# Float64 weights to float32 on VectorE and ScalarE, and exponentials with a per-partition bias, in an mLSTM cell with a GELU feed-forward block

## The chip, the cores and the metric

The kernel runs on one core of one Trainium2 chip. The metric is the device time of one execution in microseconds (us), the median of several runs. Five engines work side by side, each through its own list of instructions in order: TensorE (PE: matmuls, with weight loads in a row of their own, PEld), VectorE (DVE), ScalarE (ACT), GpSimd (POOL) and SyncE (SP). SP does no arithmetic here; it issues DMAs. They wait for one another by semaphores.

## The reference, cut to what matters

```python
# q, k, v, o_gate: (4, 8, 768, 40); i_gate, f_gate: (4, 8, 768); w_in (320, 2048), w_out (2048, 320) in float64
for t in range(S):
    m_new  = np.maximum(f[:, :, t] + m, i[:, :, t])
    f_stab = np.exp(f[:, :, t] + m - m_new)
    i_stab = np.exp(i[:, :, t] - m_new)
    m = m_new
    C = f_stab * C + i_stab * outer(v_t, k_t)          # 40 x 40 for each batch and head
    n = f_stab * n + i_stab * k_t
    y[:, :, t] = sigmoid(o_t) * (C @ q_t) / max(abs(n @ q_t), 1)
x = y as (4 * 768 tokens, 320)
out = gelu_exact(x @ w_in) @ w_out                     # float32
```

## The kernel before, in words

The 768 tokens of each of 4 batches are cut into 6 chunks of 128. A *token tile* is one chunk of one batch, 128 tokens on the partitions, 8 heads beside each other. With `M_t` the running maximum of the chunk and `a_s` the gate of token s less the sum of the forget gates, a token s weighs `exp(a_s - M_t)` for a token t at or after it.

The start (lines 126 to 182) computes `a` and `M` with one row a head, writes `M` to DRAM (`M_d`, line 164) and reads it back broadcast to all partitions, one token tile at a time (`load_M`, tile `Mb`, 512 KB, three buffers). Transposes on PE turn `a` into `aT`, tokens on the partitions.

Then come 6 chunks. Each has a *cell stage* (`cell_steps`) and a *feed-forward block*: the *up stage* (`up_steps`, line 358: 16 blocks `f` of 3 matmuls each, then GELU on ACT into `g`) and the *down part* (`down_steps`, line 371, 16 pieces of 4 matmuls). The function `weave` spreads the steps of one list between those of another: the down part of chunk c is woven into the cell stage of chunk c + 1. That is the order in which instructions stand on each engine; no engine changes its order at run time.

The cell stage has for each batch b: `turn` (k and q transposed on PE into `pt`, copied by ACT to `kT` and `qT`), `scores` (PE `ps`, then DVE multiplies `ps` by the weights `W`, line 289; PE `pf`, `pc`; the state), `values` (PE `ph`, DVE and POOL make `y`; then `load` fetches a later tile), `turn_y` (`y` transposed into `xT`, the input of the up stage). They run with a lag of one step from each to the next.

The weights `W` are made in two functions outside the steps. `distances` (line 246), ahead of the up stage, subtracts on DVE (line 251), masks on POOL (line 253) and loads the next `M`. `activations` (line 257), ahead of the cell stage, takes the exponentials of 4 token tiles (ACT, 128x1024 each, line 260) and the sigmoids of 4 output gates (line 263).

The feed-forward weights come in float64 and become float32 from their bits, in pieces (`convert`, line 212): 12 pieces of `w_in` of up to 128x512, woven into the first cell stage, and 16 of `w_out` of 128x320, woven into the first up stage. A piece takes one ACT instruction (line 222), three on POOL (lines 223 to 225) and five on DVE (lines 227 to 234). `fetch` brings the bits in, two buffers:

```python
nc.scalar.activation(out=s, in_=hf, func=AF.Abs)
nc.gpsimd.tensor_scalar(out=s, in0=s, scalar1=TINY, scalar2=None, op0=OP.is_ge)
nc.gpsimd.tensor_tensor(out=s, in0=s, in1=hf, op=OP.mult)
nc.gpsimd.tensor_scalar(out=s, in0=s, scalar1=-HUGE, scalar2=HUGE, op0=OP.max, op1=OP.min)
```

Of the kernel before, what the change touches and what calls it, by code (L numbers as in the profile page):

```python
# [36 lines left out]
def kernel(  # L37
# [32 lines left out]
    WP = 512  # L70
# [6 lines left out]
    outp = ctx.enter_context(tc.tile_pool(name="outp", bufs=3))  # L77
# [115 lines left out]
    def weight_steps():  # L193
        """What brings w_in and w_out in, a piece of at most WP columns a step."""
# [17 lines left out]
        def convert(i):  # L212
# [33 lines left out]
    def distances(c):  # L246
        """M_t - a_s for the chunk's weights exp(a_s - M_t); beyond the diagonal, what gives 0."""
        for b in range(B):
            n = c * B + b
            W[n] = wts.tile([P, H, L], F32, name="W", tag="W")  # L250
            nc.vector.tensor_tensor(out=W[n], in0=Mb.pop(n), in1=per_head(aT, c, b).to_broadcast([P, H, L]),  # L251
                                    op=OP.subtract)
# [172 lines left out]
```

## Time and profile before

| what | value |
|---|---|
| time, median of 3 runs | 833.14 us (832.2 to 833.54) |
| span of the profiled execution | 830.5 us, from its first instruction to its last |
| what lies around the span | 2.6 us, the median less the span |
| PE busy | 674.7 us, 81% of the span |
| DVE, ACT, POOL busy | 240.7, 170.4, 199.5 us |
| chain of work that ended last | PE 67%, POOL 13%, issue 11%, ACT 5% of the span |

The chain is followed back from the last instruction: at each step to what released it. Granted clock is what the throttle gave TensorE, as a share of 2.4 GHz; its other level is 1.2 GHz, 0.50. Idle time of an engine that is not the bottleneck costs nothing, so what counts is where PE stands still and what ends each of its waits.

### The profile page before, as it was taken

To read this page: it belongs to the slowest core of one execution; us is meant where nothing else is said; L and a number is where in the kernel's file an instruction comes from. 1 tells how busy PE (TensorE), PEld (TensorE's weight loads), DVE (VectorE), ACT (ScalarE), POOL (GpSimd) and SP (SyncE) were. 2 spreads that over 40 slices of the span, in tenths; PEclk is the share of its full clock that TensorE was granted. 3 is DMA by queue.
4 is the path that set the end of the run, shared out by engine and by line. 5 is a ranking of instruction groups with operands and counts; after the bars stand their busy time and mean duration, and the time that the engine had idled before them with its cause. 6 is when DMAs were issued, how large, how long until landed. Compare 5 with 4: busy or idle time off the path is not lost.

```text
span 830.5 us, 7094 instructions
## 1 busy us (share of the span) xinstructions
PE 674.7 (81%) x2714; PEld 394.8 (48%) x2714; DVE 240.7 (29%) x438; ACT 170.4 (21%) x288; POOL 199.5 (24%) x214
## 2 busy tenths in 40 slices
PE   2136424477579999799999799997999997999998
PEld 1125321122258733388533587333885335773365
DVE  4257554455534320034400144200344001330000
ACT  1411002111330022510223300225102234012200
POOL 2276654766612130011300021300113000000000
PEclk9975556788879999999999899998999998999999
DMA  9944371522204540024500035400221000000000
GB/s 141 248 80 95 66 120 29 148 64 63 63 9 66 79 110 0 0 41 66 133 23 1 6 64 82 109 0 1 41 40 41 1 0 9 9 17 0 0 9 24
DMA packets 132208, 43.47 MB, mean 52 GB/s; under 512 B 101104, under 2 KB 128752, under 8 KB 132176
## 3 DMA queue, kind: packets, MB, share of 16 engines
q1 hardware_dynamic: 132176, 43.04, 25.7%
q8 instruction: 21, 0.34, 0.2%
q14 instruction: 11, 0.09, 0.0%
HBM read 38.99 MB, written 4.03 MB: 52 GB/s over the span
## 4 chain that ended last, share of the span: by engine, by line
PE 67%; POOL 13%; issue 11%; ACT 5%; DVE 1%; DMA 1%; SPq 0%; POOLq 0%; ACTq 0%
PE pu L358 28%; PE po L371 25%; POOL sig L225 4%; PE ph L321 4%; POOL sig L223 4%; POOL sig L224 3%; PE ps L286 3%; PE pf L293 3%; ACT W L260 2%; PE pt L273 2%; PE pc L305 2%; POOL W L253 1%; ACT ob L263 1%; PE px L341 1%; ACT L263 1%
## 5 line engine op out<-in xcount | busy, mean ns | idle before, releaser
L358 PE MATMUL pu<-xT,w_in 128*128 128x512 f32 (+1 forms) x576 | 296.2, 646 | 36.4 <-ACT g L359 20.8
L371 PE MATMUL po<-w_out,g 128*128 128x320 f32 x768 | 228.5, 445 | 0.0
L358 PEld LDWEIGHTS pu<-xT,w_in 128*128 128x128 f32 (+1 forms) x576 | 96.6, 193 | 233.2 <-issue 189.8
L371 PEld LDWEIGHTS po<-w_out,g 128*128 128x128 f32 x768 | 143.6, 196 | 51.2 <-issue 5.0
L289 DVE TENSOR_TENSOR W<-ps,W 128x512 f32<-128x512 f32 x48 | 30.9, 685 | 293.5 <-PE ps L286 293.5
L359 ACT ACTIVATE g<-pu 128x512 f32<-128x512 f32 x96 | 57.1, 594 | 187.2 <-PE pu L358 187.2
L314 POOL TENSOR_TENSOR state<-state,dec 64x164 f32<-64x164 f32 x32 | 14.7, 461 | 241.5 <-PE pf L293 240.3
L273 PE MATMUL pt<-ident,kb 128*128 128x128 f32 x96 | 19.2, 335 | 60.5 <-ACT kT L276 60.5
L328 POOL TENSOR_TENSOR y<-hs,ob 128x320 f32<-128x320 f32 x24 | 19.3, 805 | 189.0 <-DVE hs L324 164.8
L321 PEld LDWEIGHTS ph<-vb,W 128*128 128x128 f32 x384 | 53.0, 215 | 4.0 <-PE px L341 0.8
L321 PE MATMUL ph<-vb,W 128*128 128x41 f32 x384 | 51.7, 300 | 0.4 <-PE px L341 0.4
L305 PE MATMUL pc<-vw,kb 128*128 128x82 f32 x160 | 24.9, 306 | 32.2 <-POOL vw L300 32.2
L253 POOL TENSOR_SCALAR_AFFINE_SELECT W<-W 128x1024 f32<-128x1024 f32 x24 | 37.2, 1571 | 56.9 <-DVE W L251 56.9
L273 PEld LDWEIGHTS pt<-ident,kb 128*128 128x128 f32 x96 | 14.1, 173 | 69.3 <-ACT kT L276 63.5
L223 POOL TENSOR_SCALAR sig<-sig 128x320 f32<-128x320 f32 (+2 forms) x28 | 34.8, 1243 | 47.0 <-ACT sig L222 47.0
L225 POOL TENSOR_SCALAR sig<-sig 128x320 f32<-128x320 f32 (+2 forms) x28 | 44.3, 1582 | 2.5
L251 DVE TENSOR_TENSOR W<-Mb,aT 128x1024 f32<-128x1024 f32 x24 | 33.3, 1425 | 26.0 <-DMA Mb<-M_d 26.0
L227 DVE TENSOR_SCALAR pow<-sig 128x320 uint32<-128x320 uint32 (+2 forms) x28 | 15.2, 543 | 86.3 <-POOL sig L225 86.2
L305 PEld LDWEIGHTS pc<-vw,kb 128*128 128x128 f32 x160 | 22.7, 219 | 33.3 <-POOL vw L300 33.3
L374 ACT COPY o_sb<-po 128x320 f32<-128x320 f32 x24 | 10.2, 425 | 132.3 <-PE po L371 132.3
L276 ACT COPY kT<-pt 128x512 f32<-128x512 f32 x24 | 13.9, 579 | 106.5 <-PE pt L273 106.5
L222 ACT ACTIVATE sig<-bits 128x320 f32<-128x320 f32 (+2 forms) x28 | 15.6, 563 | 97.4 <-DMA bits<-in_moe_w_out_dram 66.3
(71 smaller groups left out, 453.9 us busy)
## 6 DMA issues: line engine op xcount, KB each, us to landing
Mb<-M_d SPq DMA_DIRECT2D x24, 512.0 KB, 5.3
bits<-in_moe_w_out_dram SPq DMA_DIRECT2D x16, 320.0 KB, 2.9
bits<-in_moe_w_in_dram SPq DMA_DIRECT2D x8, 512.0 KB, 3.8
qb<-in_q_dram SPq DMA_DIRECT2D x24, 160.0 KB, 4.1
kb<-in_k_dram SPq DMA_DIRECT2D x24, 160.0 KB, 4.2
vb<-in_v_dram SPq DMA_DIRECT2D x24, 160.0 KB, 4.2
ob<-in_o_gate_dram SPq DMA_DIRECT2D x24, 160.0 KB, 3.8
out_dram<-o_sb SPq DMA_DIRECT2D x24, 160.0 KB, 1.9
```

Of the source, the lines that this page charges most:

```text
L223: nc.gpsimd.tensor_scalar(out=s, in0=s, scalar1=TINY, scalar2=None, op0=OP.is_ge)
L224: nc.gpsimd.tensor_tensor(out=s, in0=s, in1=hf, op=OP.mult)
L225: nc.gpsimd.tensor_scalar(out=s, in0=s, scalar1=-HUGE, scalar2=HUGE, op0=OP.max, op1=OP.min)
L251: nc.vector.tensor_tensor(out=W[n], in0=Mb.pop(n), in1=per_head(aT, c, b).to_broadcast([P, H, L]), op=OP.subtract)
L253: nc.gpsimd.affine_select(out=W[n], in_=W[n], compare_op=OP.is_ge, fill=1.0e4, base=0, pattern=[[0, H], [1, L]], channel_multiplier=-1)
L273: nc.tensor.transpose(pt[:, p, :], src[n % NLD][:, 2 * p:2 * p + 2, :].rearrange("p h d -> p (h d)"), ident)
L289: nc.vector.tensor_tensor(out=w, in0=ps[hip], in1=w, op=OP.mult)
L305: nc.tensor.matmul(pc[:, p, :], kb[n % NLD][:, m, :].rearrange("p h d -> p (h d)"), vw[:, m, :].rearrange("p h d -> p (h d)"), start=True, ...
L321: nc.tensor.matmul(ph[:, h, :], Pm[b][:, h, :], vb[n % NLD][:, h, :], start=True, stop=True)
L358: nc.tensor.matmul(pu, w_in[0:w, cc, m], xT[0:w, cc, :], start=(cc == 0), stop=(cc == 2))
L359: nc.scalar.activation(out=g[:, f, :], in_=pu, func=AF.Gelu)
L371: nc.tensor.matmul(po, g[:, f, b * L:(b + 1) * L], w_out[:, f, :], start=(f == 0), stop=(f == NF - 1))
```

## The change

The conversion of a piece leaves POOL. The sign, the exponent and the significand are now taken from the bits by DVE (lines 224, 229, 231, 232, 234 of the changed kernel), and the exponent is shifted and clamped by two Relu instructions on ACT whose bias is a column of constants (lines 226 and 227). A piece of `w_in` is up to 1024 columns wide, so there are 6 of them; those of `w_out` stay 128x320. The first chunk of `M` is written as soon as it is there, by a DMA that ACT issues, and ACT also issues the first three `load_M`. `distances` and `activations` are gone: `weights_of` masks `Mb` in place on POOL and takes the exponential of each head (128x128) with `aT` as the bias of its partition, and its step, as that of the sigmoids, stands behind the first `turn` of the cell stage. In the first chunk each sigmoid stands in `values`. The loads of `q`, `k`, `v` and `o_gate` of the first tiles are spread between the weights' fetches, and `o_sb` has 2 buffers in place of 3.

```diff
-    WP = 512
+    WP = 1024
-    for n in range(B):
-        load(n)
+    nc.vector.memset(e_hi, 1151.0 * I23)
+    nc.vector.memset(e_lo, 255.0 * I23)
...
+        if c == 0:
+            nc.scalar.dma_start(out=M_d[:, 0:L], in_=M[:, 0])
+            for n in range(NM):
+                load_M(n, nc.scalar)
-    nc.sync.dma_start(out=M_d, in_=M.rearrange("p c l -> p (c l)"))
-    for n in range(NM):
-        load_M(n)
+    nc.scalar.dma_start(out=M_d[:, L:S], in_=M[:, 1:NCH].rearrange("p c l -> p (c l)"))
...
-            nc.scalar.activation(out=s, in_=hf, func=AF.Abs)
-            nc.gpsimd.tensor_scalar(out=s, in0=s, scalar1=TINY, scalar2=None, op0=OP.is_ge)
-            nc.gpsimd.tensor_tensor(out=s, in0=s, in1=hf, op=OP.mult)
-            nc.gpsimd.tensor_scalar(out=s, in0=s, scalar1=-HUGE, scalar2=HUGE, op0=OP.max, op1=OP.min)
-            nc.vector.tensor_scalar(out=pu, in0=su, scalar1=3, scalar2=0x3F800000,
-                                    op0=OP.logical_shift_left, op1=OP.bitwise_and)
-            nc.vector.scalar_tensor_tensor(out=pu, in0=su, scalar=0xC0000000, in1=pu,
-                                           op0=OP.bitwise_and, op1=OP.bitwise_or)
-            nc.vector.tensor_scalar(out=su, in0=su, scalar1=0xFFFFF, scalar2=0x100000,
+            nc.vector.tensor_scalar(out=pu, in0=hi, scalar1=20, scalar2=0x7FF,
+                                    op0=OP.logical_shift_right, op1=OP.bitwise_and)
+            nc.scalar.activation(out=p, in_=pu, func=AF.Relu, scale=-I23, bias=e_hi[0:w])
+            nc.scalar.activation(out=pu, in_=p, func=AF.Relu, scale=-1.0, bias=e_lo[0:w])
+            nc.vector.tensor_scalar(out=su, in0=hi, scalar1=0xFFFFF, scalar2=0x100000,
                                     op0=OP.bitwise_and, op1=OP.bitwise_or)
             nc.vector.scalar_tensor_tensor(out=s, in0=lo, scalar=2.0 ** -32, in1=su, op0=OP.mult, op1=OP.add)
+            nc.vector.scalar_tensor_tensor(out=pu, in0=hi, scalar=0x80000000, in1=pu,
+                                           op0=OP.bitwise_and, op1=OP.bitwise_or)
             nc.vector.scalar_tensor_tensor(out=dst, in0=s, scalar=2.0 ** -20, in1=p, op0=OP.mult, op1=OP.mult)
             fetch(i + 2)
+            if i < n_in and i % 2 == 0:
+                load(3 + i // 2)
...
+    def weights_of(n):
+        c, b = divmod(n, B)
+        W[n] = wts.tile([P, H, L], F32, name="W", tag="W")
+        M_n = Mb.pop(n)
+        nc.gpsimd.affine_select(out=M_n, in_=M_n, compare_op=OP.is_ge, fill=1.0e30, base=0,
+                                pattern=[[0, H], [1, L]], channel_multiplier=-1)
+        for h in range(H):
+            nc.scalar.activation(out=W[n][:, h, :], in_=M_n[:, h, :], func=AF.Exp, scale=-1.0,
+                                 bias=aT[:, c, b * H + h:b * H + h + 1])
+        load_M(n + NM)
...
+            if t == 0:
+                steps.append(lambda: [weights_of(c * B + b) for b in range(B)])
+                if c > 0:
+                    steps.append(lambda: [output_gate(c * B + b) for b in range(B)])
```

How the order on the engines moves, at three places. First ACT at the start of the program. Before:

```order
L172 ACT_TABLE_LOAD
L172 ACTIVATE ew<-ew 32x640
L173 ACTIVATE gg<-gg 32x640
L260 ACTIVATE W<-W 128x1024 x4
L263 ACT_TABLE_LOAD
```

and in the changed kernel (`pow` is the exponent's buffer in `convert`):

```order
L164 DMA M_d<-M 32x128
L122 DMA Mb<-M_d 128x8x128 x3
L170 DMA M_d<-M 32x640
L175 ACT_TABLE_LOAD
L175 ACTIVATE ew<-ew 32x640
L176 ACTIVATE gg<-gg 32x640
L277 COPY kT<-pt 128x512
L277 COPY qT<-pt 128x512
L259 ACTIVATE W<-Mb,aT 128x128 x32
```

The DMAs of `M` and the first copies of `kT` and `qT` now stand ahead of the exponentials; the sigmoids (with their table load) have gone to a later place.

Second, ACT where an up stage (16 GELUs) ends and a later cell stage begins. Before:

```order
L359 ACTIVATE g<-pu 128x512 x16
L260 ACT_TABLE_LOAD
L260 ACTIVATE W<-W 128x1024 x4
L263 ACT_TABLE_LOAD
L263 ACTIVATE ob_122<-ob_122 128x320
```

and in the changed kernel:

```order
L369 ACTIVATE g<-pu 128x512 x16
L277 COPY kT<-pt 128x512
L277 COPY qT<-pt 128x512
L259 ACT_TABLE_LOAD
L259 ACTIVATE W<-Mb,aT 128x128 x32
L264 ACT_TABLE_LOAD
```

The copies of batch 0 come first, and 32 small exponentials stand where 4 large ones did; the copies of batch 1 still stand behind all of them and the sigmoids.

Third, PE at the start of the second cell stage (`kb`, `qb`: the loaded k and q of one token tile). Before:

```order
L273 MATMUL pt<-ident,kb_112 128x128 x4
L273 MATMUL pt<-ident,qb_106 128x128 x4
L371 MATMUL po<-w_out,g 128x320 x4
L273 MATMUL pt<-ident,kb_113 128x128 x4
L273 MATMUL pt<-ident,qb_107 128x128 x4
L371 MATMUL po<-w_out,g 128x320 x4
L286 MATMUL ps<-qT,kT 128x128 x8
```

and in the changed kernel:

```order
L274 MATMUL pt<-ident,kb_114 128x128 x4
L274 MATMUL pt<-ident,qb_108 128x128 x4
L381 MATMUL po<-w_out,g 128x320 x8
L274 MATMUL pt<-ident,kb_115 128x128 x4
L274 MATMUL pt<-ident,qb_109 128x128 x4
L381 MATMUL po<-w_out,g 128x320 x4
L289 MATMUL ps<-qT,kT 128x128 x8
L296 MATMUL pf<-state_100,qT 128x82 x4
L308 MATMUL pc<-vw,kb_114 128x82 x4
L381 MATMUL po<-w_out,g 128x320 x4
L274 MATMUL pt<-ident,kb_110 128x128 x4
```

Two groups of the down part, not one, now stand between the first two `turn`s, since the two new steps draw one each. The `pt` buffers are two, so each `turn` waits until ACT has copied the one before it out.

## Rows read from the trace of the kernel before

**Rows 1.** Busy time by stage: stretch, length, PE, PEld, DVE, ACT, POOL, clock, DMA, GB/s.

```profile
39.80:136.10 96.30, 35.95 (x189) 32.13 (x188) 56.31 (x95) 10.28 (x19) 58.90 (x41) 0.57 0.47 83
136.10:215.90 79.80, 58.94 (x96) 18.48 (x96) 39.64 (x70) 16.35 (x32) 52.93 (x47) 0.81 0.29 84
215.90:291.60 75.70, 61.58 (x366) 48.48 (x366) 32.13 (x66) 16.05 (x28) 19.60 (x26) 0.91 0.30 51
291.60:338.80 47.20, 47.20 (x97) 15.30 (x95) 3.85 (x3) 10.66 (x17) 6.41 (x5) 1.00 0.18 48
338.80:405.30 66.50, 60.46 (x366) 47.85 (x366) 21.54 (x46) 15.18 (x26) 9.46 (x16) 0.97 0.29 48
...
348.10:350.20 2.10, 2.08 (x9) 2.09 (x10) 0.00 (x0) 1.06 (x3) 0.00 (x0) 0.50 0.00 0
```

**Rows 2.** Groups by line and shape in the first cell stage, 39.8 to 136.1 us.

```profile
L225 POOL TENSOR_SCALAR sig<-sig 128x512 f32<-128x512 f32 x8 | 16.1, 2010 | 0.7
...
L231 DVE TENSOR_SCALAR sig<-sig 64x512 uint32<-64x512 uint32 x3 | 1.3, 419 | 0.1
```

**Rows 3.** Timeline in the first up stage: start, length, engine, line; one piece of `w_out`.

```profile
178.68 0.67 DVE L233 SCALAR_TENSOR_TENSOR sig<-bits,sig 128x320 f32<-128x320 uint32 x1
...
179.87 0.33 DVE L227 TENSOR_SCALAR pow<-sig 128x320 uint32<-128x320 uint32 x1
180.23 0.49 DVE L229 SCALAR_TENSOR_TENSOR pow<-sig,pow 128x320 uint32<-128x320 uint32 x1
...
182.41 0.48 ACT L222 ACTIVATE sig<-bits 128x320 f32<-128x320 f32 x1 [6.73 <-DMA bits<-in_moe_w_out_dram]
```

**Rows 4.** Timeline of the start: `M`, the gates on ACT, `pt`, and SP's DMAs.

```profile
5.67 0.47 DVE L160 TENSOR_TENSOR_SCAN M<-a,m 32x128 f32<-32x128 f32 x1
...
11.07 0.74 ACT L173 ACTIVATE gg<-gg 32x640 f32<-32x640 f32 x1
...
14.63 1.06 PE L273 MATMUL pt<-ident,qb 128*128 128x128 f32 x4
...
17.07 1.09 SPq L164 DMA_DIRECT2D M_d<-M  x1
20.66 11.18 SPq L123 DMA_DIRECT2D Mb<-M_d  x7
```

**Rows 5.** Timeline where the second up stage ends and a cell stage begins.

```profile
338.93 0.60 ACT L359 ACTIVATE g<-pu 128x512 f32<-128x512 f32 x1 [2.37 <-PE pu L358]
...
339.76 2.32 PE L371 MATMUL po<-w_out,g 128*128 128x320 f32 x8
340.84 3.89 ACT L260 ACTIVATE W<-W 128x1024 f32<-128x1024 f32 x4
...
346.05 1.55 ACT L263 ACTIVATE ob<-ob 128x320 f32<-128x320 f32 x4
347.50 0.56 ACT L276 COPY kT<-pt 128x512 f32<-128x512 f32 x1
...
348.12 1.11 PE L273 MATMUL pt<-ident,kb 128*128 128x128 f32 x4 [6.04 <-ACT kT L276]
```

**Rows 6.** Single lines and one tile over the whole span: lengths in ns; `Mb`'s landing in us.

```profile
L343 ACT COPY xT<-px x24: 258/258/260, 91.7 to 743.7; 64x128 f32<-64x128 f32 x24
...
L251 DVE TENSOR_TENSOR W<-Mb,aT x24: 1209/1220/2108, 24.6 to 639.1; 128x1024 f32<-128x1024 f32 x24
...
L253 POOL TENSOR_SCALAR_AFFINE_SELECT W<-W x24: 1086/1092/3150, 25.9 to 640.4; 128x1024 f32<-128x1024 f32 x24
...
DMA to landing us min/median/max: 3.7/5.3/8.0
```

**Rows 7.** Timeline of DVE in the first cell stage: what one batch takes beside the conversion.

```profile
80.98 1.28 DVE L289 TENSOR_TENSOR W<-ps,W 128x512 f32<-128x512 f32 x2
82.18 0.65 DVE L311 COPY state<-pc 64x164 f32<-64x164 f32 x2
...
89.12 0.50 DVE L326 COPY hs<-ph 128x328 f32<-128x328 f32 x1
...
91.28 0.42 DVE L342 COPY xT<-px 128x256 f32<-128x256 f32 x1
```

More of the change, by code (lines that the diff above doesn't have):

```diff
@@ L15 @@
 P = 128
-TINY = 3.4332275390625e-05
-HUGE = 122879.9921875
+I23 = 2.0 ** 23
 def weave(main, fill):
@@ L76 @@
     two = ctx.enter_context(tc.tile_pool(name="two", bufs=2))
-    outp = ctx.enter_context(tc.tile_pool(name="outp", bufs=3))
+    outp = ctx.enter_context(tc.tile_pool(name="outp", bufs=2))
     dram = ctx.enter_context(tc.tile_pool(name="dram", bufs=1, space=bass.MemoryType.DRAM))
@@ L90 @@
     ident = const.tile([P, P], F32, name="ident")
+    e_hi = const.tile([P, 1], F32, name="e_hi")
+    e_lo = const.tile([P, 1], F32, name="e_lo")
     last = const.tile([P, P], F32, name="last")
@@ L115, with load_M @@
     Mb, W = {}, {}
-    def load_M(n):
+    def load_M(n, eng=nc.sync):
         if n >= NCH * B:
@@ L122, in load_M @@
         Mb[n] = wts.tile([P, H, L], F32, name="Mb", tag="Mb", bufs=NM)
-        nc.sync.dma_start(out=Mb[n], in_=M_d[b * H:(b + 1) * H, c * L:(c + 1) * L]
-                          .unsqueeze(0).to_broadcast([P, H, L]))
+        eng.dma_start(out=Mb[n], in_=M_d[b * H:(b + 1) * H, c * L:(c + 1) * L]
+                      .unsqueeze(0).to_broadcast([P, H, L]))
     nc.sync.dma_start(out=f_sb.rearrange("p c l -> p (c l)"), in_=f_gate.rearrange("b h s -> (b h) s"))
     nc.sync.dma_start(out=i_sb.rearrange("p c l -> p (c l)"), in_=i_gate.rearrange("b h s -> (b h) s"))
-    for t in qb[0:B] + kb[0:B]:
+    load(0)
+    for t in kb[0:B] + qb[0:B]:
         nc.gpsimd.memset(t[:, :, D:DP], 0.0)
@@ L216, in convert @@
             lo, hi = x[:, :, 0], x[:, :, 1]
-            hf = hi.bitcast(F32)
-            s = raw.tile([P, WP], F32, name="sig", tag="sig")[0:w, 0:n]
+            s = raw.tile([P, WP], F32, name="sig", tag="sig", bufs=1)[0:w, 0:n]
             p = raw.tile([P, WP], F32, name="pow", tag="pow")[0:w, 0:n]
             su, pu = s.bitcast(U32), p.bitcast(U32)
-            nc.scalar.activation(out=s, in_=hf, func=AF.Abs)
-            nc.gpsimd.tensor_scalar(out=s, in0=s, scalar1=TINY, scalar2=None, op0=OP.is_ge)
-            nc.gpsimd.tensor_tensor(out=s, in0=s, in1=hf, op=OP.mult)
-            nc.gpsimd.tensor_scalar(out=s, in0=s, scalar1=-HUGE, scalar2=HUGE, op0=OP.max, op1=OP.min)
-            nc.vector.tensor_scalar(out=pu, in0=su, scalar1=3, scalar2=0x3F800000,
-                                    op0=OP.logical_shift_left, op1=OP.bitwise_and)
-            nc.vector.scalar_tensor_tensor(out=pu, in0=su, scalar=0xC0000000, in1=pu,
-                                           op0=OP.bitwise_and, op1=OP.bitwise_or)
-            nc.vector.tensor_scalar(out=su, in0=su, scalar1=0xFFFFF, scalar2=0x100000,
+            nc.vector.tensor_scalar(out=pu, in0=hi, scalar1=20, scalar2=0x7FF,
[3 more added lines that the diff above has]
+            nc.vector.tensor_scalar(out=su, in0=hi, scalar1=0xFFFFF, scalar2=0x100000,
                                     op0=OP.bitwise_and, op1=OP.bitwise_or)
             nc.vector.scalar_tensor_tensor(out=s, in0=lo, scalar=2.0 ** -32, in1=su, op0=OP.mult, op1=OP.add)
+            nc.vector.scalar_tensor_tensor(out=pu, in0=hi, scalar=0x80000000, in1=pu,
+                                           op0=OP.bitwise_and, op1=OP.bitwise_or)
             nc.vector.scalar_tensor_tensor(out=dst, in0=s, scalar=2.0 ** -20, in1=p, op0=OP.mult, op1=OP.mult)
             fetch(i + 2)
+            if i < n_in and i % 2 == 0:
+                load(3 + i // 2)
         fetch(0)
+        load(1)
         fetch(1)
+        load(2)
         steps = [lambda i=i: convert(i) for i in range(len(pieces))]
@@ L244, in per_head, with output_gate @@
         return t[:, c, b * H:(b + 1) * H].unsqueeze(2)
[L246 to L252, printed above, removed]
-            nc.gpsimd.affine_select(out=W[n], in_=W[n], compare_op=OP.is_ge, fill=1.0e4, base=0,
-                                    pattern=[[0, H], [1, L]], channel_multiplier=-1)
-            load_M(n + NM)
-    def activations(c):
-        for b in range(B):
-            n = c * B + b
-            nc.scalar.activation(out=W[n], in_=W[n], func=AF.Exp, scale=-1.0)
-        for b in range(B):
-            t = ob[(c * B + b) % NLD]
-            nc.scalar.activation(out=t, in_=t, func=AF.Sigmoid)
+    def weights_of(n):
[8 more added lines that the diff above has]
+        load_M(n + NM)
+    def output_gate(n):
+        nc.scalar.activation(out=ob[n % NLD], in_=ob[n % NLD], func=AF.Sigmoid)
     def cell_steps(c):
@@ L279, in scores @@
             n = c * B + b
+            if n not in W:
+                weights_of(n)
             Pm[b] = W.pop(n)
@@ L318, in values @@
             n = c * B + b
+            if c == 0:
+                output_gate(n)
             ph = ps_h.tile([P, H, D1], F32, name="ph", tag="h")
@@ L377, in down_steps @@
         return [lambda b=b, f=f: part(b, f, f + 4) for b in range(B) for f in range(0, NF, 4)]
-    distances(0)
     in_steps, out_steps = weight_steps()
-    for n in range(B, NLD):
-        load(n)
-    activations(0)
     weave(cell_steps(0), in_steps)
     for c in range(NCH):
-        if c + 1 < NCH:
-            distances(c + 1)
         g = gp.tile([P, NF, TG], F32, name="g", tag="g")
@@ L390 @@
         if c + 1 < NCH:
-            activations(c + 1)
             weave(cell_steps(c + 1), down_steps(c, g))
```

## The prediction

> **What bounds the kernel now.** I read the stages first [rows 1], since a share over the whole span hides where the time lies. An up stage in its steady form is PE and nothing else: 47.2 us, all busy, clock 1.00. The first up stage takes 79.8 us for the same work, and the first cell stage 96.3 us with PE busy for 36.0 at a mean clock of 0.57. In both POOL is the busiest of the others, 58.9 and 52.9 us. The groups say with what: one of POOL's three conversion instructions alone takes 2.01 us for 512 columns [rows 2]. In the chain of waits these stages go through POOL's conversion and the waits around it, one piece behind the other. Later cell stages (five; the first of them 75.7 us, the others some 66.5) have one hole each: PE waits 6.04 us for ACT's copy of `kT`, because exponentials and sigmoids stand ahead of it [rows 5], and then runs 2.1 us at clock 0.50, the 1.2 GHz level [rows 1]. So the change meets three places: the way to the first up matmul (136.15 us into the span), the first up stage, and the holes.
>
> **The way to the first up matmul.** The chain is now on ACT, then DVE.
> - The scan of the first chunk of `M` ends at 6.14 [rows 4]. Before, `M_d` was issued at 17.07 and the first `Mb` could follow at 20.66, 3.6 us later. From 6.2 that puts the first `Mb` at 9.8; three issues by ACT at up to 1.1 each and the second `M_d` keep ACT until about 12.5. A table load of 1.3 (the gap from the GELU's end to the first exponential [rows 5]) and `ew`, `gg` at 0.74 each give 15.3; before, `gg` ended at 11.81 and the second `pt` at 15.69, 3.9 later, so 19.2 now, and two copies of 0.56 end at 20.3. The first `Mb` lands 3.7 to 8.0 us after its issue [rows 6], POOL masks it in 1.09: 14.6 to 18.9, covered.
> - An exponential of 128 columns has no row. Bounds: a copy of 64x128 takes 0.258 alone [rows 6]; an eighth of the 1024-wide one is 0.12 and a 320-wide sigmoid, back to back, 0.39 [rows 5]. I take 0.26, the same width: 2.1 a token tile. The fourth tile needs a buffer of the three, so its `Mb` is issued when the first tile's exponentials end (22.4), lands a median 5.3 later, is masked by 28.8, and its exponentials end at 30.9; those of tiles 2 and 3 lie inside. Copies of the second batch 1.1, then the two Relus of piece 0, by the 1024-wide rate of 3.89/4 and some 0.1 for the hand-over 1.06 each: 34.1. DVE, which did its first steps meanwhile, goes on here.
> - From there DVE is in order and the bound. The last two instructions of piece 0 at 1.22 (a two-source operation 1024 wide [rows 6]): 2.4. Four batches at 1.85 for scores and state and 2.58 from `hs` to the end of `xT` [rows 7]: 17.7. Pieces 1 to 4: a bit operation with one source took 0.33 us for 320 and 0.42 for 512 columns [rows 2, 3], about 0.7 for 1024; then the Relus 2.2 with the hand-over, with two DVE instructions beside them; then 2.4: 5.5 each, 22.0. If reading every second word costs the one-source operation its rate, it takes 1.22 and a piece 6.2. I take 5.5 and keep 6.2 for the range. PE runs its `ps` and `pc` between these at half clock, and DVE waits for it at batch 1 and 2; 3 us. ACT's last `xT` 0.3. Sum: 34.1 + 2.4 + 17.7 + 22.0 + 3 + 0.3 = 79.5, some 56.5 us earlier.
>
> The Trainium skill, VectorE: DVE Perf Modes, What auto-detection actually checks, lets a single-source operation run two elements a cycle if source and destination are in SBUF, and names no stride; by it a piece is the 5.5. No row here has a strided one.
>
> **The first up stage.** PE needs 47.2. The clock is low before it; 2.1 us at half rate [rows 1] cost 1.1. A piece of `w_out` on DVE and ACT: 0.33 to 0.49 for the first instruction, two Relus of 0.48 to 0.55, two DVE instructions of 0.49 [rows 3] and five hand-overs of under 0.1: 2.6 to 2.9, and a buffer of bits comes back 3.06 us after it is freed (179.35 to 182.41 [rows 3]) for every two pieces. PE's block of three matmuls takes 47.2/16 = 2.95, so PE is the bound, by little; 1.5 us for friction. 49.8 against 79.8: 30.0 earlier. POOL's 52.9 us there fall away with no heir on the path.
>
> **The holes.** Count from the end of an up stage. ACT: the GELU ends at 0.7 [rows 5], copies of batch 0 1.1, table 1.3, four tiles of exponentials; the fourth `Mb` is again issued behind the first tile (at 5.2), lands at 10.5, is masked at 11.6, and its exponentials end at 13.7. Then 2.8 for the table and sigmoids (344.73 to 347.50 [rows 5]) and the copy: 17.1. PE meanwhile has two `turn`s of 0.94 (338.83 to 339.76 for the first), four groups of the down part at 2.2 [rows 5], `ps`, `pf`, `pc` 2.9: 13.6 before it needs that copy. So the wait is 3.5 in place of 6.04; part of it moves forward, to `pc`, as POOL's `vw` now stands behind the fourth mask. The slow clock behind it I leave as it is, 1.1. That is 2.5 for each of the four later cell stages, 10. The second cell stage is 75.7 long, 9.2 over the steady 66.5, for ACT was held by the last conversion; now the last two Relus hold it for 1.0. Gain 9.2 - 1.0 + 2.5 = 10.7.
>
> **Other edits.** SP's four `Mb` loads stand ahead of bits 2 and the fourth tile's loads, so these wait for ACT until 30.9; they are needed on DVE and PE from about 45 on. Two `o_sb` buffers suffice, as the four copies are a group of several us apart from the landing. DVE's `distances` lay beside an up stage bound by PE and cost nothing before.
>
> **Sum.** 56.5 + 30.0 + 10 + 10.7 = 107.2. The profiled span is 830.5, with 2.6 to the median: 833.1 - 107.2 = 725.9; I say 726.
>
> **The rivals.**
> - *Small exponentials are dear* (0.39 each, the sigmoid's price). Tiles take 3.1; in a hole ACT reaches the copy at about 19, PE waits 5.4 and the gain there is 0.6 at most: 9.5 less over five stages, the start 2 to 4 later. 739. The copy of the same width at 0.258 speaks against it; that the bias is now a column in SBUF speaks for it. The Trainium skill, ScalarE: Activation LUTs, What ACT_TABLE_LOAD costs, gives 93 ns more for such a bias and 280 ns + 0.833 ns a column in all, less 93 ns back to back; by it, as an estimate, an exponential takes 0.29, and the sum would be 5 us higher. The same table of rules tells authors to keep Relu off ScalarE; nothing before shows a Relu.
> - *Conversion remains the bound.* If ACT's GELU comes between the Relus of a piece and the loop takes 3.5 to 3.9, the up stage is 9 to 15 us longer, and with pieces of 6.2 the start 3: 738 to 744.
> - *The early `M` is hidden anyway*: `Mb` queues behind 1 MB of bits and lands as late as before. First mask near 25, the chain above 5 to 6 later: 732.
> - *The holes close* (exponentials near 0.13, DMA at its shortest 3.7). ACT reaches the copy at about 14; the waits and the slow clock go, 3.5 more for each of five stages, and 2 at the start: 707.
> - *Slower than before*: Relu on 32-bit integers runs at a fraction of the float rate. With a factor k each wide piece takes 2.1 (k - 1) more and each narrow one 1.0 (k - 1) beyond the slack of 0.2; five wide pieces on the path and 16 narrow ones eat 107 us at k near 5.2. At k = 6 the time is about 855. Every row of ACT goes by columns whatever the function, and DVE reads such integers at the float rate; I see no sign of it.
>
> **How the numbers follow.** My forecast, 720 to 732 us, 0.40; dear exponentials 0.20; conversion still the bound 0.14; `M` hidden 0.13; holes closed 0.11; slower 0.02. The range 708 to 744 leaves out the last two and the ends of the second rival. Faster by over 0.2% (1.7 us, what a measurement of this kernel can tell) 0.97, the same 0.01, slower 0.02.
>
> **What would show it.** After, the first up matmul should start at 76 to 84 us, no POOL instruction should stand between the masks and `vw`, `y` and the state, the first up stage 48 to 52 with PE busy throughout, and each later cell stage one or two waits of 3 to 4 us in sum ahead of the third `turn`. PE waiting for GELU between blocks of the first up stage would show the second rival; a wait of 6 us would show the first; the first mask behind 20 us the third. The forecast is wrong as a whole if the first up matmul comes later than 95 us.

## The result, and the profile after

The changed kernel takes 721.89 us (median of 4 runs, 721.42 to 722.26) against 832.9 us for the kernel before on the same chip: a ratio of 0.8672, 95% interval 0.866 to 0.8685. 726 was predicted. The span of the profiled execution went from 830.5 to 720.2 us, 110.3 less.

| stretch (us of the span) | before | predicted | after |
|---|---|---|---|
| start to first up matmul | 136.15 | 79.5 | 84.14 |
| first up stage | 79.8 | 49.8 | 51.7 |
| second cell stage | 75.7 | 65.0 | 62.7 |
| each later cell stage but the last | 66.3 to 67.5 | 64.0 | 61.8 to 62.1 |
| last cell stage | 63.9 | 61.4 | 60.8 |

Busy times by stage of the changed kernel, with the columns of [rows 1]: stretch, length, PE, PEld, DVE, ACT, POOL, clock, DMA, GB/s. The first line is the rest of the first cell stage, then come the first up stage, the second cell stage and a later one.

```profile
37.00:84.10 47.10, 28.74 (x156) 26.08 (x156) 41.16 (x63) 14.33 (x20) 8.44 (x9) 0.54 1.01 155
84.10:135.90 51.80, 51.76 (x97) 16.86 (x98) 34.35 (x82) 27.94 (x50) 0.00 (x0) 0.92 0.44 112
135.90:198.50 62.60, 59.29 (x364) 46.65 (x365) 22.00 (x48) 21.54 (x56) 14.15 (x20) 1.00 0.39 84
245.90:307.80 61.90, 59.34 (x365) 46.73 (x365) 20.34 (x44) 20.64 (x54) 14.16 (x20) 1.00 0.41 85
```

POOL has nothing in the first up stage, where it had 52.93 us, and PE is busy throughout. Ahead of it DVE is now the busiest, 41.16 of 47.10 us.

The start of the changed kernel, in the timeline (start, length, engine, line; in brackets the idle time before and what ended it):

```profile
6.12 0.36 ACTq L164 DMA_DIRECT2D M_d<-M  x1
11.53 3.09 ACTq L122 DMA_DIRECT2D Mb<-M_d  x3
14.66 1.81 ACTq L170 DMA_DIRECT2D M_d<-M  x1
16.50 1.28 ACT L175 ACT_TABLE_LOAD   x1 [16.50 <-DMA Mb<-M_d]
16.82 1.09 POOL L256 TENSOR_SCALAR_AFFINE_SELECT Mb<-Mb 128x1024 f32<-128x1024 f32 x1 [10.02 <-DMA Mb<-M_d]
23.56 7.11 ACT L259 ACTIVATE W<-Mb,aT 128x128 f32<-128x128 f32 x24
26.07 7.78 SPq L122 DMA_DIRECT2D Mb<-M_d  x4
30.98 2.45 ACT L259 ACTIVATE W<-Mb,aT 128x128 f32<-128x128 f32 x8 [0.31 <-POOL Mb L256]
34.27 1.15 ACT L226 ACTIVATE pow<-pow,e_hi 128x1024 f32<-128x1024 uint32 x1
36.64 1.22 DVE L232 SCALAR_TENSOR_TENSOR pow<-bits,pow 128x1024 uint32<-128x1024 uint32 x1 [12.48 <-ACT pow L227]
```

The chain is the predicted one: `M_d`, `Mb`, ACT's exponentials, the fourth tile's `Mb`, the Relus, DVE. An exponential takes 7.11/24 = 0.296 us. ACT stands at its own DMA issues until 16.50, and only then loads its table.

One wide piece on DVE in the first cell stage of the changed kernel, undisturbed, in the timeline:

```profile
45.18 0.69 DVE L224 TENSOR_SCALAR pow<-bits 128x1024 uint32<-128x1024 uint32 x1
45.79 0.69 DVE L229 TENSOR_SCALAR sig<-bits 128x1024 uint32<-128x1024 uint32 x1
46.51 1.23 DVE L231 SCALAR_TENSOR_TENSOR sig<-bits,sig 128x1024 f32<-128x1024 uint32 x1
48.27 1.22 DVE L232 SCALAR_TENSOR_TENSOR pow<-bits,pow 128x1024 uint32<-128x1024 uint32 x1 [0.54 <-ACT pow L227]
49.53 1.22 DVE L234 SCALAR_TENSOR_TENSOR w_in<-sig,pow 128x1024 f32<-128x1024 f32 x1
```

From 45.18 to 50.75 it takes 5.6 us; 5.5 was predicted. And the end of that stage, where POOL begins the second chunk's masks:

```profile
75.34 3.88 POOL L256 TENSOR_SCALAR_AFFINE_SELECT Mb<-Mb 128x1024 f32<-128x1024 f32 x3
75.42 1.35 DVE L339 TENSOR_TENSOR y<-y,den 128x320 f32<-128x320 f32 x1 [0.52 <-POOL y L333]
76.70 1.57 DVE L224 TENSOR_SCALAR pow<-bits 128x1024 uint32<-128x1024 uint32 x1
78.19 1.57 DVE L229 TENSOR_SCALAR sig<-bits 128x1024 uint32<-128x1024 uint32 x1
84.14 1.22 PE L368 MATMUL pu<-xT,w_in 128*128 128x512 f32 x1 [6.35 <-DVE xT L347]
```

The same two bit operations that took 0.69 take 1.57 while masks run. PE waits 6.35 us for the `xT` copy that stands behind this piece.

A later cell stage of the changed kernel, which answers to [rows 5]:

```profile
256.49 2.45 ACT L259 ACTIVATE W<-Mb,aT 128x128 f32<-128x128 f32 x8 [0.42 <-POOL Mb L256]
257.21 1.12 PE L308 MATMUL pc<-vw,kb 128*128 128x82 f32 x8 [0.77 <-POOL vw L303]
262.32 0.66 PE L274 MATMUL pt<-ident,kb 128*128 128x128 f32 x4 [1.79 <-ACT kT L277]
```

Two waits, 0.77 and 1.79, have taken the place of one of 6.04, and the transposes of `k` behind them take 0.66 us where they took 1.11 [rows 5]: the granted clock stays at 1.00 over the stage. The last cell stage is another case:

```profile
590.46 0.66 PE L274 MATMUL pt<-ident,kb 128*128 128x128 f32 x4 [3.66 <-ACT kT L277]
```

It has no `pc`, so there is one wait of 3.66, and the group of the down part behind it takes 3.71 us where it takes 2.32 in the stage above.

### The profile page after: what moved, and what is told of

It is laid out like the page before. It is cut to its first block, busy times and chain, and to the rows that moved or that the text cites. A ratio compares the mean times of both kernels' runs of the same rounds, so it can differ in the third digit from the quotient of the medians.

```text
span 720.2 us, 7040 instructions
## 1 busy us (share of the span) xinstructions
PE 658.3 (91%) x2714; PEld 385.3 (53%) x2714; DVE 187.5 (26%) x386; ACT 218.9 (30%) x472; POOL 81.3 (11%) x130
## 3 DMA queue, kind: packets, MB, share of 16 engines
q10 hardware_dynamic: 3216, 1.67, 1.0%
## 4 chain that ended last, share of the span: by engine, by line
PE 78%; ACT 10%; DVE 5%; DMA 4%; POOL 1%; issue 1%; ACTq 1%; POOLq 0%; SPq 0%; DVEq 0%
PE pu L368 40%; PE po L381 23%; PE ph L326 5%; ACT W L259 4%; DMA Mb<-M_d 3%; PE ps L289 3%; PE pf L296 2%; PE pc L308 2%; PE pt L274 2%; ACT ob L264 1%; POOL Mb L256 1%; PE px L346 1%; ACT L264 1%; ACT L259 1%; DVE pow L232 1%
## 5 line engine op out<-in xcount | busy, mean ns | idle before, releaser
L368 PE MATMUL pu<-xT,w_in 128*128 128x512 f32 (+1 forms) x576 | 288.9, 633 | 6.3 <-DVE xT L347 6.3
L381 PE MATMUL po<-w_out,g 128*128 128x320 f32 x768 | 223.0, 438 | 0.0
L381 PEld LDWEIGHTS po<-w_out,g 128*128 128x128 f32 x768 | 141.0, 192 | 50.1 <-issue 1.7
L256 POOL TENSOR_SCALAR_AFFINE_SELECT Mb<-Mb 128x1024 f32<-128x1024 f32 x24 | 27.4, 1161 | 322.8 <-DMA Mb<-M_d 322.8
L259 ACT ACTIVATE W<-Mb,aT 128x128 f32<-128x128 f32 x192 | 57.4, 387 | 2.4 <-POOL Mb L256 2.3
L289 PE MATMUL ps<-qT,kT 64*128 64x128 f32 x384 | 31.2, 304 | 3.9 <-DVE W L292 3.9
L348 ACT COPY xT<-px 64x128 f32<-64x128 f32 x24 | 6.2, 258 | 93.2 <-DVE xT L347 93.1
L289 PEld LDWEIGHTS ps<-qT,kT 64*128 64x128 f32 x384 | 26.2, 204 | 14.1 <-issue 9.7
L329 DVE TENSOR_TENSOR hs<-ph,far 128x328 f32<-128x328 f32 x20 | 10.0, 499 | 54.5 <-PE ph L326 54.5
L317 POOL TENSOR_TENSOR state<-state,dec 64x164 f32<-64x164 f32 x32 | 14.7, 460 | 76.9 <-PE pf L296 75.7
L232 DVE SCALAR_TENSOR_TENSOR pow<-bits,pow 128x320 uint32<-128x320 uint32 (+2 forms) x22 | 15.2, 691 | 31.4 <-ACT pow L227 31.4
```

Of the source, the lines that this page charges most:

```text
L232: nc.vector.scalar_tensor_tensor(out=pu, in0=hi, scalar=0x80000000, in1=pu, op0=OP.bitwise_and, op1=OP.bitwise_or)
L256: nc.gpsimd.affine_select(out=M_n, in_=M_n, compare_op=OP.is_ge, fill=1.0e30, base=0, pattern=[[0, H], [1, L]], channel_multiplier=-1)
L259: nc.scalar.activation(out=W[n][:, h, :], in_=M_n[:, h, :], func=AF.Exp, scale=-1.0, bias=aT[:, c, b * H + h:b * H + h + 1])
L289: nc.tensor.matmul(ps[hip][:, p, :], kT[b][r, p, :], qT[b][r, p, :], start=True, stop=True)
L368: nc.tensor.matmul(pu, w_in[0:w, cc, m], xT[0:w, cc, :], start=(cc == 0), stop=(cc == 2))
L381: nc.tensor.matmul(po, g[:, f, b * L:(b + 1) * L], w_out[:, f, :], start=(f == 0), stop=(f == NF - 1))
```

## The experiments

The first four take the change apart. Medians are of 4 or 5 runs; the second value is the ratio to the kernel before on the same chip. The kernel before took 831.5 to 832.9 us on the chips used, so two medians from different chips that lie 1.4 us apart tell nothing.

**Exponentials and sigmoids back ahead of the cell stage** (`e1_old_place`).

```diff
-            if t == 0:
-                steps.append(lambda: [weights_of(c * B + b) for b in range(B)])
-                if c > 0:
-                    steps.append(lambda: [output_gate(c * B + b) for b in range(B)])
...
+            activations(c + 1)
             weave(cell_steps(c + 1), down_steps(c, g))
```

> The changed kernel, but the exponentials and sigmoids stand ahead of the cell stage again, where they stood before; they stay small and with a bias. Theory (the place matters: what ACT does ahead of the first copies of kT and qT is a wait of PE): ACT works some 15 us in each later cell stage before the copy PE needs, PE has 3.2 us of work, so the wait is about 12 us and a stage 72 in place of 62; about 770 us. Rival (the cell stages are shorter because DVE's subtraction is gone or the weights are made otherwise, not for the place): 722 us, within 3.

Measured: 775.73 us, 0.9324 [0.9308, 0.934], 54 us above the change. One later cell stage in its timeline:

```profile
380.16 7.11 ACT L259 ACTIVATE W<-Mb,aT 128x128 f32<-128x128 f32 x24
393.39 1.12 PE L274 MATMUL pt<-ident,kb 128*128 128x128 f32 x4 [11.98 <-ACT kT L277]
```

The hole is 11.98 us, twice that of before, since 32 small exponentials hold ACT for 9.6 us where 4 large ones took 3.89 [rows 5]. So the small exponentials are dear in themselves; only their place behind the first copies makes them cheap for PE. The 4 large ones at the new place were not tried.

**M written whole, by SP** (`e2_whole_M_on_SP`).

```diff
-            nc.scalar.dma_start(out=M_d[:, 0:L], in_=M[:, 0])
-            for n in range(NM):
-                load_M(n, nc.scalar)
...
-    nc.scalar.dma_start(out=M_d[:, L:S], in_=M[:, 1:NCH].rearrange("p c l -> p (c l)"))
+    nc.sync.dma_start(out=M_d, in_=M.rearrange("p c l -> p (c l)"))
+    for n in range(NM):
+        load_M(n)
```

> The changed kernel, but M is written whole by SP behind the first tile's loads, and SP issues the first three Mb, not ACT. Theory A (sending the first M early is no gain: ACT stands at its own DMA issues until 16.5 us and its gate exponentials, the transposes and the first copies wait behind them): the copies end near 17 in place of 23.6, the exponentials start near 21 with the first masked Mb; 719 to 720 us. Theory B (the early M sets the start): M leaves 3.4 us later and all follows; about 725 us.

Measured: 726.66 us, 0.8737 [0.872, 0.8753], 4.8 above the change. Its start:

```profile
9.56 0.33 SPq L165 DMA_DIRECT2D M_d<-M  x1
15.15 1.09 POOL L253 TENSOR_SCALAR_AFFINE_SELECT Mb<-Mb 128x1024 f32<-128x1024 f32 x1 [8.34 <-DMA Mb<-M_d]
16.28 7.12 ACT L256 ACTIVATE W<-Mb,aT 128x128 f32<-128x128 f32 x24
29.72 9.39 SPq L122 DMA_DIRECT2D Mb<-M_d  x4
36.24 2.45 ACT L256 ACTIVATE W<-Mb,aT 128x128 f32<-128x128 f32 x8 [12.84 <-POOL Mb L253]
```

Though `M` is written 3.4 us later, the first mask comes 1.7 earlier than in the change and the first exponentials 7.3 earlier, as ACT issues no DMA. The loss is at the fourth tile: SP reaches its `Mb` at 29.72, not 26.07, behind weights and loads that now stand later in its queue, and it lands 1.6 us later than that besides (5.4 us from issue to mask, not 3.8); ACT waits 12.84 us. So the early `M` pays by what it takes off SP's queue, not by the first mask.

**The conversion alone** (`e3_conversion_alone`): the kernel before with the new instructions of `convert`, pieces still 512 wide, nothing else.

> The kernel before with the new conversion (no GpSimd) and nothing else, pieces of 512 columns. Theory (most of the gain is the conversion): the first up matmul near 102 us in place of 136, the first up stage 52 in place of 80, the second cell stage some 8 shorter, later ones as before; about 763 us. Rival (the start and the place of the exponentials carry most): above 790 us.

Measured: 759.28 us, 0.9124 [0.9107, 0.914]: some 73 of the 111 us. The first up stage in its timeline:

```profile
96.99 10.80 PE L357 MATMUL pu<-xT,w_in 128*128 128x512 f32 x18 [6.30 <-DVE xT L341]
109.55 3.04 PE L357 MATMUL pu<-xT,w_in 128*128 128x512 f32 x6 [1.76 <-ACT g L358]
112.79 35.67 PE L357 MATMUL pu<-xT,w_in 128*128 128x512 f32 x72 [0.20 <-ACT g L358]
```

39.2 us come from the start (136.15 to 96.99) and 28.3 from the up stage (79.8 to 51.5).

**Pieces of 512 columns in the changed kernel** (`e4_narrow_pieces`).

```diff
-    WP = 1024
+    WP = 512
...
-            if i < n_in and i % 2 == 0:
-                load(3 + i // 2)
+            if i < n_in and i % 4 == 1:
+                load(3 + i // 4)
```

> The changed kernel with w_in in pieces of 512 columns as before. Theory (fixed costs and the hand-over to ACT and back are paid per piece): about 3.4 us for a piece of 512, 6.8 for what takes 5.7 as one piece, five of these on the path; 726 to 728 us. Rival (finer pieces interleave better with the cell's own work): 722 us or less.

Measured: 729.01 us, 0.877 [0.8749, 0.879], 7 above the change. Half a piece in its timeline:

```profile
48.51 0.43 DVE L224 TENSOR_SCALAR pow<-bits 128x512 uint32<-128x512 uint32 x1
50.48 0.69 DVE L232 SCALAR_TENSOR_TENSOR pow<-bits,pow 128x512 uint32<-128x512 uint32 x1 [0.48 <-ACT pow L227]
```

The wait for ACT is 0.48 for 512 columns and 0.54 for 1024, so a narrow piece pays nearly the same wait for half the work: 3.4 us (48.51 to 51.92) against 5.6. The first up matmul comes at 92.07.

The next runs ask where the prediction's start, up stage and holes were off.

**PE kept busy ahead of the first up stage** (`e5_warm`; eight matmuls whose result is not used).

```diff
+    for r in range(2):
+        warm = ps_mm.tile([P, TG], F32, name="warm", tag="mm")
+        for cc in range(4):
+            nc.tensor.matmul(warm, w_in[:, 0, 0:P], w_in[:, 1, 0:TG], start=(cc == 0), stop=(cc == 3))
     for c in range(NCH):
```

> The changed kernel with 8 extra matmuls of 512 columns, whose result is not used, on PE ahead of the first up stage, in the 6.35 us in which PE waits for xT. Theory (the first up stage is 4.4 us longer than the steady 47.3 because of the granted clock at its start): that stage takes 48 to 49 us, total 718 to 719. Rival (its excess is the conversion of w_out on DVE and ACT): stage 51 to 52, total 722 or up to 1 more.

Measured: 722.28 us, 0.8685 [0.8673, 0.8697], the same. Its PE timeline:

```profile
78.15 9.39 PE L394 MATMUL warm<-w_in 128*128 128x512 f32 x16
87.38 47.43 PE L368 MATMUL pu<-xT,w_in 128*128 128x512 f32 x96
```

The stage takes 47.43 us, as the steady ones do, with the same conversion beside it: all 4.3 us of its excess are the clock's. In the trace of the change its first 10.06 us have a mean granted clock of 0.57 and the rest 1.00; here it is 1.00 throughout. The gain was paid elsewhere. The filler ran at 0.50 until 82.6 (by the windows of this trace) and went on to 87.38, 3.2 us past the start that the change had, and some 1 us more lies in the later cell stages (the third takes 62.4 in place of 61.9, the last 61.3 in place of 60.8).

**POOL's masks held until the first GELU** (`e6_masks_later`).

```diff
+    def hold_pool(g):
+        hold = two.tile([P, 1], F32, name="hold", tag="hold", bufs=1)
+        nc.gpsimd.tensor_copy(out=hold, in_=g[:, 0, 0:1])
...
+        if c == 0:
+            hold_pool(g)
```

> The changed kernel with the second chunk's masks on POOL held until the first GELU is there. Theory (in the last wide piece on the path the two one-source DVE instructions take 1.57 us in place of 0.69, and the y product 1.35 in place of 0.67, because POOL's three masks run at that moment): these go back to 0.69 and 0.67, the first up matmul comes 2.4 us earlier; about 719.5 us. Rival (those lengths have another cause, such as SP's DMAs): 722 us.

Measured: 717.52 us, 0.8629 [0.8617, 0.8641], 4.4 below the change; its trace, of the slowest of the four runs, is 3.1 below. From its timeline:

```profile
76.11 0.69 DVE L224 TENSOR_SCALAR pow<-bits 128x1024 uint32<-128x1024 uint32 x1
82.40 49.67 PE L372 MATMUL pu<-xT,w_in 128*128 128x512 f32 x96 [5.19 <-DVE xT L351]
```

Without masks beside them the bit operations are back at 0.69 and the `y` product is at 0.49 (not 0.67, which it takes beside POOL's `vw`), 2.6 us less for the three. The start is 1.7 us earlier, not 2.4, since DVE's wait of 0.54 for the Relus, which the longer operations had covered, is back. Another 2.1 us of the trace lie in the first up stage, 49.67 in place of 51.72. That part is not shown to be the masks' doing: five other runs of this list, with other edits and with the masks where the change has them, have a stage of 49.2 to 49.7 too.

**Four buffers for `Mb`** (`e7_four_M_buffers`; for room, one buffer for the exponents).

```diff
-    NM = 3
+    NM = 4
...
-            p = raw.tile([P, WP], F32, name="pow", tag="pow")[0:w, 0:n]
+            p = raw.tile([P, WP], F32, name="pow", tag="pow", bufs=1)[0:w, 0:n]
```

> The changed kernel with four buffers for Mb in place of three (and one for pow in place of two, for the room). Theory (the fourth tile's M, which waits for the first tile's exponentials, costs each later cell stage 0.42 us on ACT, and 0.77 of PE's waits move with it): 0.4 us off each of five stages; 719 to 721 us. Rival (the fourth load is what the stage waits for): 2.5 us off each of five, about 710 us.

Measured: 722.88 us, 0.8692 [0.867, 0.8714], no difference that this can tell. Its start and one later cell stage:

```profile
11.65 4.98 ACTq L122 DMA_DIRECT2D Mb<-M_d  x4
19.08 1.28 ACT L175 ACT_TABLE_LOAD   x1 [19.08 <-DMA Mb<-M_d]
38.80 1.22 DVE L232 SCALAR_TENSOR_TENSOR pow<-bits,pow 128x1024 uint32<-128x1024 uint32 x1 [11.21 <-ACT pow L227]
```

In the cell stage `pc` no longer waits, but `kT`'s wait grows to 2.6 (13.1 us over five stages). At the start the fourth issue holds ACT 2.6 us longer; DVE goes on 2.2 later, and the first up matmul is at 88.26, 4.1 later. Most of the other 1.9 is POOL again: it now has four masks, 5.37 us, beside the last piece on the path, whose first two two-source instructions take 1.99 and 1.75 in place of 1.22. One gain and one loss; neither the theory's 719 to 721 nor the rival's 710 came.

**Sigmoids behind the second `turn`** (`e8_gates_later`).

```diff
+            if t == 1 and c > 0:
+                steps.append(lambda: [output_gate(c * B + b) for b in range(B)])
             if t == 0:
                 steps.append(lambda: [weights_of(c * B + b) for b in range(B)])
-                if c > 0:
-                    steps.append(lambda: [output_gate(c * B + b) for b in range(B)])
```

> The changed kernel with the sigmoids of the later chunks behind the second turn and the first scores. Theory (PE's wait of 1.79 us ahead of the third turn is ACT's way to the second copies; the sigmoids and their table load are 2.8 us of it): that wait goes in each of five stages, about 713 us. Rival (the sigmoids then hold up the third copies and a wait of the same size comes one step later): 722 us.

Measured: 727.0 us (726.01 to 731.88), 0.8768 [0.8744, 0.8792], 5 above the change. A later cell stage in its timeline:

```profile
369.11 2.00 PE L308 MATMUL pc<-vw,kb 128*128 128x82 f32 x8 [3.19 <-POOL vw L303]
```

The step taken away drew one group of the down part with it, so PE reaches `pc` some 2.2 us earlier, counted from the stage's start, and waits there: 3.19. The wait for `kT` is gone, but behind this one `pc` runs at half rate (2.00 for what takes 1.12 above), and so does the group of the down part behind it. These stages get about 3 us longer. In the last cell stage, which has no `pc`, the same edit saved 4.4 (60.8 to 56.4). A version with it in that stage alone was not tried.

The last four look for a faster version. In the change the fifth piece of `w_in` stands ahead of the last `xT` copy, but its columns are first read in the ninth block of the up stage.

**The last wide pieces in the up stage** (`e9_last_piece_later`).

```diff
-    weave(cell_steps(0), in_steps)
+    weave(cell_steps(0), in_steps[:5])
+    out_steps = [lambda: None, in_steps[5], lambda: None] + out_steps
```

> Edit: the change, but the fifth piece of w_in (its columns are not read before the ninth block of the up stage) stands behind the last turn_y, and the sixth behind the second block of the first up stage. Theory: DVE, in order, is the bound of the last stretch; the last px is done at 77.8 in the trace of the change, and its copy waits for the piece in front until 83.3, so the first up matmul comes some 5.5 us earlier (77 to 80), the stage stays within 1 us of 51.7, and the median is 715 to 718. Rival: the first up stage has no room for more conversion; the GELUs stand behind Relus that wait for a wide piece (5.0 us on DVE against 2.95 of a block on PE), PE waits 4 to 6 us there, and the median stays at 720 to 723.

Measured: 717.2 us (714.9 to 720.42), 0.8624 [0.8602, 0.8645].

```profile
78.69 51.68 PE L368 MATMUL pu<-xT,w_in 128*128 128x512 f32 x96 [0.52 <-DVE xT L347]
134.69 0.57 ACT L277 COPY kT<-pt 128x512 f32<-128x512 f32 x1
145.30 2.00 PE L308 MATMUL pc<-vw,kb 128*128 128x82 f32 x8 [4.42 <-POOL vw L303]
```

Both held in part. The start is 5.45 us earlier and the stage no longer, as the theory had it. But the stage ends at 130.37, and ACT still has Relus of `w_out` in front of `kT`'s first copy at 134.69; `pc` waits 4.42 us there, the second cell stage takes 66.8 us in place of 62.7, and 4.1 are given back. This trace is of the slowest of the five runs (720.42); the others, at 714.9 to 718.08, gave back less than it did.

**Three pieces there, and the masks later still** (`e10_pieces_and_masks`): `in_steps[:4]`, and `hold_pool` on the seventh GELU. **The same with two unused matmuls ahead of the last `px` groups** (`e11_and_warm`).

> Edit: as the one before, but three pieces of w_in stand in the first up stage (the fourth right behind the last turn_y, the others behind blocks 2 and 4), and POOL holds the second chunk's masks until the seventh GELU. Theory: two wide pieces of some 5.5 us and the collision of 2.4 leave the way to the first up matmul: 70 to 74; the stage takes 52 to 54, since three wide pieces of 5.0 and sixteen narrow ones of 2.1 fill DVE for 49 us; median 707 to 712. Rival: DVE is then the bound of the stage, each wide piece holds a GELU for longer than PE's two buffers cover, the stage takes 58 or more, and the median is 715 to 720.

> Edit: as the one before, with one unused matmul of 512 columns ahead of each of the last two px groups, in the waits that PE has there. Theory: what the first up stage takes over 47.3 us beside waits is the low granted clock after a stretch with waits; with PE busy in these waits the stage comes 1.5 to 4.3 us shorter at the same start, and the median is 1.5 to 4 below the one before. Rival: two short fillers do not lift the clock, or they hold px up by their own 1.7 us each: the median is the same or up to 2 above.

Measured: 724.21 us, 0.8714 [0.8696, 0.8732], and 724.11 us, 0.871 [0.8696, 0.8725]. The first of the two:

```profile
47.47 1.08 PE L278 MATMUL pt<-ident,kb 128*128 128x128 f32 x4 [6.11 <-DMA kb<-in_k_dram]
51.45 1.29 DVE L296 TENSOR_TENSOR W<-ps,W 128x512 f32<-128x512 f32 x2 [5.91 <-PE ps L293]
78.93 29.14 PE L372 MATMUL pu<-xT,w_in 128*128 128x512 f32 x54 [0.52 <-DVE xT L351]
110.00 24.14 PE L372 MATMUL pu<-xT,w_in 128*128 128x512 f32 x42 [1.94 <-ACT g L373]
```

Taking a further piece from DVE moved the first up matmul by nothing (78.93 after 78.69). PE waits 6.11 us for the fourth tile's `k`, a DMA that SP issues behind the first piece, and DVE stands idle for 5.91 us behind it, since no piece stands at that place of its list now. The last version below has the same wait (6.04) with a piece there and starts at 75.49, so the wait alone did not cost the gain. The stage grows to 55.2 with a wait for GELU, short of the rival's 58, and the second cell stage to 67.4; the total is worse than the rival's 715 to 720. The two fillers changed neither the start nor the stage: the theory of the second run falls for fillers this short.

**Both, with the tail in view** (`e12_both`).

```diff
-    weave(cell_steps(0), in_steps)
+    weave(cell_steps(0), in_steps[:5])
+    two_pieces = lambda: (out_steps[6](), out_steps[7]())
+    up_fill = in_steps[5:] + out_steps[:6] + [two_pieces] + out_steps[8:]
...
+        if c == 0:
+            hold_pool(g)
```

> Edit: the masks of the second chunk held until the first GELU, the fifth piece of w_in behind the last turn_y, the sixth behind the first block of the up stage, and two pieces of w_out behind one block in the middle, so that no more than one piece is left for the end of the stage. Theory: the run with the last piece later gained 5.5 us at the start and lost 4.1 in the second cell stage, because ACT still had Relus of w_out in front of kT's first copy when the up stage ended; with that tail gone the first up matmul is at 77.5 to 79, kT's first copy stands within 2 us of the end of the up stage, the second cell stage takes 62.5 to 64, and the median is 711 to 715. Rival: the tail comes from the conversion's total work in the up stage, not from its order; the copy is again more than 3 us late, and the median is 716 to 719.

Measured: 714.5 us (711.63 to 715.84), 0.8571 [0.8552, 0.859], against 0.8672 [0.866, 0.8685] for the change: faster than both kernels.

```profile
75.49 52.13 PE L372 MATMUL pu<-xT,w_in 128*128 128x512 f32 x96 [0.52 <-DVE xT L351]
82.12 5.15 POOL L256 TENSOR_SCALAR_AFFINE_SELECT Mb<-Mb 128x1024 f32<-128x1024 f32 x3
82.15 2.13 DVE L231 SCALAR_TENSOR_TENSOR sig<-bits,sig 64x1024 f32<-64x1024 uint32 x1
129.20 0.56 ACT L281 COPY kT<-pt 128x512 f32<-128x512 f32 x1
139.79 2.00 PE L312 MATMUL pc<-vw,kb 128*128 128x82 f32 x8 [1.67 <-POOL vw L307]
```

The up stage ends at 127.62 and `kT`'s copy stands at 129.20, within the 2 us of the theory: the tail was a matter of order. The start is earlier than the theory had it (77.5 to 79), and the second cell stage takes 64.0: its wait of 1.67 is followed by half rate. The masks still slow DVE (2.13 us for 1.22), now where PE is covered.

## Why the prediction was right, and where its terms were off

The total is 4 us from the forecast, and that is in part luck: the mechanism of each part held, but the start and the first up stage gained 6.4 us less than forecast and the cell stages 9.7 more, and these errors cancelled.

- *The way to the first up matmul*, 56.5 us predicted, 52.0 measured. Its chain and its order held, and so did the piece at 5.5 (5.6). Two terms failed. First, "from 6.2 that puts the first `Mb` at 9.8" and "ACT until about 12.5": `M_d` took 5.3 us to land, so `Mb` was issued at 11.53, and four DMA issues held ACT until 16.5. (Three issues at the prediction's own bound of 1.1 each would have ended at 13.1, with the second `M_d` still to come.) Exponentials at 0.296 (0.26 taken) and Relus at 1.15 (1.06) added to it, a landing of the fourth `Mb` in 3.8 and not 5.3 gave back: DVE went on at 36.64, not 34.1. Second, a term that was not there: POOL's masks of the second chunk start as soon as the last `y` leaves POOL and lengthen three DVE operations by 0.86 + 0.88 + 0.88 = 2.6 us, of which 0.54 fell on a wait for the Relus; with the masks held, the start was 1.7 earlier. A row had a sign of it: in [rows 6] DVE's subtraction takes 1220 ns at the median and up to 2108, and in that trace one of 1.97 us starts at 28.34, 0.2 us after one of POOL's masks.
- *The first up stage*, 30.0 predicted, 28.1 measured. PE is busy throughout and the conversion has room, as forecast (ACT waits 1.33 us for PE in 14 of the 16 blocks). The friction of 1.5 was not there; the clock's 1.1 was 4.3, as the fillers showed. The price of 2.1 us at half rate [rows 1] was the wrong row: it followed a single hole, and here PE had run at a mean clock of 0.54 for the 47 us ahead. No run shows how to get the size from that: behind a like stretch six other versions have an excess of 1.8 to 2.2.
- *The holes*, 10 predicted for four, some 17.4 measured (4.4, 5.3, 4.5 and, in the last, 3.1). Of the 4.4 of the third cell stage 3.5 are waits (6.04 to 2.56; 3.5 were left by the prediction). ACT reached the copy 0.7 us sooner than forecast, as the fourth mask ended 10.6 us into the stage and not at 11.6, and PE had 0.3 more to do. The rest is the step "the slow clock behind it I leave as it is": with waits of 0.77 and 1.79 the clock did not fall. The last cell stage, with one wait of 3.66, and the run with one of 3.19 show the other case, at half rate behind it. The second cell stage gained 13.0 for 10.7 in the same way: a wait of 14.12 fell to 1.51 and 1.79.
- *The rivals.* Dear exponentials fell: 0.296 back to back, not 0.39. Conversion as the bound fell: no wait for GELU in the up stage. The early `M` was not hidden: the first mask is at 16.82, and without it the time is 4.8 us more, though by SP's queue and not by the first mask. Of "the holes close" the clock's part came true by another way, shorter waits and not their end. Relu on integers runs at a float operation's rate: 1.15 us for 1024 columns, where a GELU of 512 takes 0.60.

The Trainium skill, ScalarE: Activation LUTs, What ACT_TABLE_LOAD costs, gave an estimate of 0.29 us for an exponential; the trace agrees, at 0.296. The Trainium skill, VectorE: DVE Perf Modes, What auto-detection actually checks, lets a single-source operation from SBUF to SBUF, with the outermost dimensions both even or equal, run two elements a cycle; the trace agrees for a strided source: 0.69 us for 1024 columns against 1.22 for two sources.

## What to carry to other kernels

Before moving work off a busy engine, look for what it will start earlier: the masks that POOL now reached at once fell on the very DVE operations that bounded the stage. An instruction that is dear by itself can be right if it stands where its engine is awaited by nobody, so price the place and not only the operation. In a stage that converts weights, put ahead of the first use only what the first use reads, and check that no tail is left in front of the next stage's first copy.

## What the runs showed of the hardware that was not expected

- A DVE bit operation with one source went from 0.69 to 1.57 us, and one with two sources from 1.22 to 2.13, while POOL masked tiles; POOL's masks went from 1.09 to a mean of 1.29 beside the first and 1.72 beside the second. Each DVE excess, 0.88 and 0.91, is below one mask's length. The Trainium skill, SBUF — State Buffer, Who interferes with whom, says that the two engines share a pair of ports, and that of a DVE instruction in a two-port mode and a GpSimd instruction the one that comes second waits for the other's whole instruction; the excess of the one-source operation agrees with that. That the masks are the cause is shown by the run that held them; that the ports are is not shown by a run.
- Reading every second 32-bit word cost DVE's one-source operation nothing: 0.31 to 0.33 us for 320 columns and, in the run with narrow pieces, 0.43 for 512, against 0.33 and 0.42 for words that lie side by side [rows 2, 3]; for 1024 it took 0.69, where the two-source operation beside it took 1.22.
- A 16 KB write to DRAM took 5.3 us to land at the start, beside 1 MB of weights in flight, and each issue of an `Mb` load held ACT for about a microsecond (3.09 for three; 4.98 for four with four buffers).
- The 96 matmuls of the first up stage, with PE always busy, took 47.4 us in one version, 49.2 to 49.7 in six and 51.7 to 52.1 in three, by how long they ran at half clock; and a wait of 1.67 us was followed by half rate in the last version, one of 1.79 in the change was not. What decides between these is left open.
